# A Fourier layer and a two-layer net on one core: half tiles first, eight weight parts converted in eleven steps, and zero products in TensorE's first pauses

## The chip, the core and the metric

The kernel runs on one NeuronCore of a Trainium2 chip. Its engines run side by side, each through its own list of instructions, and wait for each other on semaphores: TensorE (PE, matmuls; PEld is its weight load), VectorE (DVE), ScalarE (ACT), GpSimd (POOL) and SyncE (SP, which here only issues DMAs). The metric is the device time of one execution in microseconds. Less is better. PE can be granted half its clock; the profile shows the granted share.

## The reference

```python
X = np.fft.rfft(x, axis=1)                       # x: 8 x 3008 x 256
Yr = Xr @ w_r - Xi @ w_i + b_r
Yi = Xr @ w_i + Xi @ w_r + b_i
Yr = np.sign(Yr) * np.maximum(np.abs(Yr) - 0.01, 0.0)    # Yi likewise
y = np.fft.irfft(Yr + 1j * Yi, n=3008, axis=1)
h = y.reshape(24064, 256) @ w_in                 # w_in: 256 x 2048
out = np.maximum(h, 0.0) ** 2 @ w_out            # w_out: 2048 x 256
```

Everything is in float32 but w_in and w_out, which come as float64 and are converted on the chip. A product in full float32 precision is made of two-part numbers: each operand is split into a rounded part and a rest (fp32r), and three products are added; where the operands are still plain fp32, PE runs two passes instead, and the trace has two records for one matmul.

## The kernel before

The length 3008 is 47 × 64. A batch's transform has four stages: **fwd**, 13 products of x with a 120 × 120 matrix (`Fwd`, `Fwd2`, `Fwd32`), whose results go to DRAM (`s1`); **pairs** (or single **units** for batch 0), which load 64 rows of them as `ka`, multiply by a matrix `kbb` (`kb`), mix with w_r and w_i, shrink, and multiply back with `kk` (`kcm`), with results to DRAM (`s3`) as `kuh` and `kul`; **back**, which loads `du` from `s3` and multiplies by `dx_sb` (`dm_sb` for batch 0) to make the tokens' inputs; and **tokens**, sums and splits of these into `yt`. Each batch has six token tiles of 504 or 500 tokens (`HALF`, half of it each).

The net of a tile runs in 8 **steps** of two hidden blocks (`Step`): `first` and `second` make seven products in `psh` instead of eight (a scheme of sums in the manner of Strassen, so win holds seven blocks each in two parts), DVE makes `mu`, `mv` and `mc` from them (L556, L108), ACT squares and rounds (`mg`, L104), POOL makes the rest of `mg` (L111), and `out` two half-steps later adds 12 products into `pso`. Half-steps are the unit of time of a planner (`Plan`): the other batches' transforms are groups with a wanted half-step, a number of half-steps for which they hold one of two PSUM banks (`psfa`, `psfb`), and groups that they follow; `placed` gives each the first fitting half-step. Within a half-step the order of the code is kept on each engine by `then`.

Ahead of the steps, in the order of the program: the **ring** (batch 0's fwd, seven `Fwd32` with folds of x on DVE and POOL), then the mix weights' loads, then 24 **units** in a pipeline (`r` counts them) with their back products, while DVE converts parts of the weights; then seven fwd products of batch 1 (`second`), then back products of tile 0 and 1 and two more of `second`. The 16 **parts** of w_in and w_out are each loaded (`dst`) and converted on ACT and DVE by `begin`, `sign`, `least`, `top`, `power`, `times`, `plus` (L155 to L183), and then split into two parts, for w_in together with sums of two parts (`ds`). Parts 0 to 10 go beside the units (`PACED`), parts 12 and 13 just behind (`BEHIND`), and parts 11, 14 and 15 (`LATE`) together with the sums of parts 12 and 13 in **turns**: what `late_parts` lists is put out on ACT and DVE at the start of each of the first seven steps.

SP's queue is in the order of the code; there is a rule that a load is issued only after a named instruction (`issue_after`). The loads of a unit (`Unit32.load`) are `ka`, and for each fourth unit `kbb` and `kk` (for four units) behind it.

Of the kernel before, what the change touches and what calls it, by code (L numbers as in the profile page):

```python
# [11 lines left out]
F32 = mybir.dt.float32  # L12
# [28 lines left out]
MAIN = {  # L41
    "xs": 1, "xe": 1, "du": 2, "kv": 1, "kp": 1, "kq": 1, "ksh": 1, "ksl": 1, "kxl": 1, "kxh": 1, "kyh": 1, "kyl": 1, "ke": 1, "kb": 1, "yr": 1,
    "ms": 1, "mp": 1, "mu": 1, "mv": 1, "mc": 3, "nam": 1,
}
CONV = ("big", "small", "dw", "ds")
SIDE = ("xs", "ka", "kb", "kcm", "kxh", "kxl", "kyh", "kyl", "kp", "kq", "ke", "kv", "ksh", "ksl", "kuh", "kul", "ku")
# [14 lines left out]
def fnet_moe(ctx: ExitStack, tc, x, w_r, w_i, b_r, b_i, w_in, w_out, bm, cm, dx, a32, c32, d32, out):  # L61
# [58 lines left out]
    nc.sync.dma_start(am32, a32)  # L120
    pool.memset(lam, -LAM)
    w32 = []


    def load_mix_weights():
# [18 lines left out]
    class Double:  # L144
# [7 lines left out]
        def begin(self):  # L152
            self.f = T("df", [128, 512], I32, tag="small")
# [3 lines left out]
        def sign(self):  # L157
            return dve.tensor_scalar(
# [98 lines left out]
    class Fwd:  # L257
# [28 lines left out]
        def run(self):  # L286
# [3 lines left out]
            self.ev = T("xe", [M1, 1, 2, D], F32)  # L290
# [15 lines left out]
    class Pair:  # L306
# [73 lines left out]
        def back(self, g):  # L380
            ps = bank([128, 512])
            for n, (j, r) in enumerate(((0, self.sh), (1, self.sh), (0, self.sl))):
                then(
                    pe, pe.matmul, ps[:, :D], self.cm[:, g, j * 128:(j + 1) * 128], r[:, g],
                    start=n == 0, stop=n == 2,
                )
            store_back(self.b, self.g + g, ps[:, :D])


    class Fwd2(Fwd):  # L390
        kept = None

# [8 lines left out]
        def run(self):  # L401
# [7 lines left out]
            self.ev = T("xe", [M1, 1, 2, D], F32, tag=self.kept or ("xe" if self.q >= PRE else "xf"))  # L409
# [5 lines left out]
    class Fwd32(Fwd):  # L415
# [6 lines left out]
        def mm(self):  # L422
            n = self.n
            self.ps, self.folds = [], []
            for t, eng in enumerate((dve, dve if self.alone else pool)):
# [3 lines left out]
                nc.tensor.matmul(ps[:M1, :n], am32[:, t], u[:, :n], start=True, stop=True)  # L429
# [8 lines left out]
    kk = [None, None]  # L438

    class Unit32:  # L440
        def __init__(self, b, g):
            self.b, self.g = b, g

        def load(self):
            self.a = T("ka", [128, D], F32)
            self.get = nc.sync.dma_start(self.a, s1[self.b][self.g, :N1].rearrange("n t c -> (n t) c"))
            if self.g % 4 == 0:
                with tc.issue_after(units[self.g - 4].get.ins if self.g else ring[-1].last.ins):
                    for j, (name, src) in enumerate((("kbb", bm), ("kk", c32))):
                        kk[j] = T(name, [128, 4, 128], F32)  # L450
                        nc.sync.dma_start(kk[j], src[:, self.g:self.g + 4])
            self.m, self.k = kk[0][:, self.g % 4], kk[1][:, self.g % 4]

        def fwd(self):
            self.ps = ps = bank([128, 2, 256])
            for c in range(2):
                nc.tensor.matmul(  # L457
                    ps[:, c, 0:128], self.a[:, c * 128:(c + 1) * 128], self.m, start=True, stop=True
# [22 lines left out]
        def back(self):  # L481
            self.ps = ps = bank([128, 512])
            nc.tensor.matmul(ps[:, :D], self.k, self.v, start=True, stop=True)  # L483
# [74 lines left out]
    class Tokens:  # L558
# [16 lines left out]
        def split(self, k):  # L575
            y, h = raw[self.t], self.h
            eng = pool if k == 1 else self.eng
            if k == 0:
                yts[self.t] = [
                    T(f"yt{j}", [128, 7 * HM], F32R)[:, :7 * h].rearrange("p (j h) -> p j h", j=7) for j in range(2)  # L580
# [12 lines left out]
    acc = {}  # L593

    class Step:
# [8 lines left out]
        def first(self):  # L604
# [10 lines left out]
            eng = dve if self.t else act  # L615
# [5 lines left out]
        def second(self):  # L621
# [7 lines left out]
            if self.t:  # L629
# [12 lines left out]
        def out(self, j):  # L642
            t, h, f = self.t, self.h, 2 * self.n + j
            if f == 0:
                acc[t] = [bank([128, 512], f"pso{d}") for d in range(2)]

            for d, k in ((0, 0), (0, 1), (1, 0), (1, 1), (0, 2), (1, 2)):
# [4 lines left out]
                    start=f == 0 and k == 0, stop=f == NF - 1 and k == 2,  # L652
                )
            if f == NF - 1:
                b, c0, _ = tiles[t]

# [361 lines left out]
```

## Time and profile before

| what | us |
| --- | --- |
| three runs | 2602.91, 2604.4, 2605.41 (median 2604.4) |
| profiled execution: time | 2605.25 |
| profiled execution: span of its records | 2603.5 |
| PE busy (granted clock 0.996) | 2567.4 |
| DVE, ACT, POOL busy | 1731.9, 1329.7, 1622.1 |

A row of a timeline has start and duration of instructions of one kind (us), the engine, the line, what is made from what (tile names without numbers), the shape, the count, and in brackets the idle time ahead of it with what ended it. A row of waits has the engine and line that waited, what it waited for, total us, number and longest.

### The profile page before, as it was taken

Reading aid. Unit: us, or ns where it says so; the run is one execution under the profiler, and the core shown is the slowest. Engines: PE = TensorE matmul, PEld = TensorE weight load, DVE = VectorE, ACT = ScalarE, POOL = GpSimd, SP = SyncE. Lnnn points to the kernel's source line nnn. Section 1 sums busy time; section 2 is a strip of 40 time slices with the busy share of each in tenths; the row PEclk is TensorE's granted clock in tenths of the full one; section 3 lists DMA queues with packets and bytes.
Section 4 is the critical chain, followed back from the end, with each engine's and each line's share of the span. In section 5 each row is a group of like instructions: output and inputs, shape, how many; then the busy total and the mean of one; then the engine's idle time right before and its main releaser. Section 6 shows DMA issues by size and latency. Waiting matters only on the chain.

```text
span 2603.5 us, 46919 instructions
## 1 busy us (share of the span) xinstructions
PE 2567.4 (99%) x16940; PEld 2349.0 (90%) x16940; DVE 1731.9 (67%) x3724; ACT 1329.7 (51%) x2100; POOL 1622.1 (62%) x1614
## 2 busy tenths in 40 slices
PE   7999999999999999999999999999999999999999
PEld 5889999999999999999999999999999999999998
DVE  6786666676757666576666666667666677755554
ACT  5655454554545545555455554545455555545453
POOL 1066676666766766667666766676666666656664
PEclk8999999999999999999999999999999999999999
DMA  8623333233323333233322343223332232211010
GB/s 266 218 76 101 107 92 92 84 114 103 97 70 117 99 105 94 76 97 99 112 86 82 103 119 101 74 80 107 104 110 76 67 96 92 62 47 53 21 35 17
DMA packets 184569, 244.21 MB, mean 94 GB/s; under 512 B 20910, under 2 KB 129958, under 8 KB 184338
## 3 DMA queue, kind: packets, MB, share of 16 engines
q1 hardware_dynamic: 171442, 217.10, 27.5%
q0 software_dynamic: 12896, 24.11, 3.8%
q8 instruction: 135, 2.21, 0.4%
q14 instruction: 96, 0.79, 0.1%
HBM read 143.74 MB, written 97.39 MB: 93 GB/s over the span
## 4 chain that ended last, share of the span: by engine, by line
PE 96%; DVE 2%; DMA 1%; issue 1%; POOL 0%; ACT 0%; SPq 0%; POOLq 0%; DVEq 0%; ACTq 0%
PE pso L556 39%; PE psh L556 35%; PE psfa L556 9%; PE psfb L556 9%; PE psf L471 2%; PE psf L429 1%; DMA s<-xe 1%; DVE mc L108 0%; PE psf L457 0%; PE psf L483 0%; DVE df L166 0%; PE psf L556 0%; DVE dw L177 0%; DVE da L163 0%; DVE mv L556 0%
## 5 line engine op out<-in xcount | busy, mean ns | idle before, releaser
L111 POOL TENSOR_TENSOR mg<-mc,mg 128x500 fp32r<-128x500 f32 (+1 forms) x768 | 962.8, 1275 | 671.0 <-ACT mg L104 617.7
L556 PE MATMUL pso<-mg,wout 128*128 128x500 f32 (+1 forms) x4608 | 1156.9, 391 | 0.5 <-ACT mg L104 0.2
L556 PE MATMUL psh<-yt,win 128*128 128x250 f32 (+1 forms) x8064 | 1052.3, 281 | 3.3 <-DVE mc L108 3.2
L556 PEld LDWEIGHTS psh<-yt,win 128*128 128x128 f32 x8064 | 992.4, 189 | 17.5 <-DVE mc L108 2.7
L556 PEld LDWEIGHTS pso<-mg,wout 128*128 128x128 f32 x4608 | 823.8, 188 | 135.6 <-POOL mg L111 2.6
L556 ACT ACTIVATE mc<-mc 128x1000 f32<-128x1000 f32 (+1 forms) x384 | 400.7, 1044 | 577.7 <-DVE mc L108 576.4
L108 DVE CUSTOM_DVE_ANT_0 mc<-psh,mv 128x500 f32<-128x500 f32 (+3 forms) x768 | 420.4, 548 | 383.3 <-PE psh L556 340.1
L104 ACT CAST mg<-mc 128x1000 fp32r<-128x1000 f32 (+1 forms) x384 | 396.5, 1032 | 22.4 <-ACT mc L556 1.8
L556 DVE TENSOR_TENSOR mv<-psh,mu 128x500 f32<-128x500 f32 (+1 forms) x384 | 260.8, 679 | 36.9 <-PE psfa L556 0.9
L105 DVE COPY mp<-psh 128x250 f32<-128x250 f32 (+1 forms) x376 | 157.1, 418 | 87.8 <-PE psh L556 67.4
L556 DVE TENSOR_TENSOR mu<-psh,mp 128x250 f32<-128x250 f32 (+1 forms) x384 | 160.5, 418 | 16.7 <-ACT mp L104 5.8
L268 POOL TENSOR_TENSOR xs<-xt 120x256 f32<-120x256 f32 x156 | 112.5, 743 | 80.8 <-PE psfa L556 34.0
L108 DVE CUSTOM_DVE_ANT_0 mc<-psh,mp 128x250 f32<-128x250 f32 (+1 forms) x384 | 156.7, 408 | 0.0
L111 POOL TENSOR_TENSOR ksl<-kv,ksh 128x512 fp32r<-128x512 f32 x84 | 108.9, 1297 | 16.3 <-ACT ksh L104 9.5
L111 POOL TENSOR_TENSOR yt<-ms,yt 128x500 fp32r<-128x500 f32 (+1 forms) x94 | 107.5, 1144 | 5.3 <-ACT yt L104 5.2
L111 POOL TENSOR_TENSOR yt<-yr,yt 128x500 fp32r<-128x500 f32 (+1 forms) x95 | 89.6, 943 | 10.4 <-ACT yt L104 5.5
L111 POOL TENSOR_TENSOR ms<-yr 128x250 f32<-128x250 f32 (+1 forms) x94 | 65.8, 707 | 46.3 <-DVE yr L543 41.9
L373 DVE TENSOR_TENSOR kv<-psfa,ke 64x256 f32<-64x256 f32 x148 | 62.3, 421 | 37.6 <-PE psfa L556 27.8
L373 DVE TENSOR_TENSOR kv<-psfb,ke 64x256 f32<-64x256 f32 x188 | 79.1, 421 | 12.4 <-PE psfb L556 7.0
L111 POOL TENSOR_TENSOR kyl<-kp,kyh 128x256 fp32r<-128x256 f32 x84 | 62.5, 744 | 33.2 <-ACT kyh L104 32.4
L104 ACT CAST ksh<-kv 128x512 fp32r<-128x512 f32 x84 | 52.0, 619 | 59.1 <-DVE kv L111 59.1
L556 PE MATMUL psfb<-wx,kxh 128*128 128x256 f32 x352 | 76.4, 280 | 0.0
(153 smaller groups left out, 2772.4 us busy)
## 6 DMA issues: line engine op xcount, KB each, us to landing
du<-s SPq DMA_DIRECT2D x112, 256.0 KB, 3.1
ka<-s SPq DMA_DIRECT2D x84, 256.0 KB, 3.5
kcm<-cm_in POOLq DMA_DIRECT2D x84, 256.0 KB, 3.3
s<-kuh SPq DMA_DIRECT2D x168, 128.0 KB, 1.8
s<-kul SPq DMA_DIRECT2D x168, 128.0 KB, 2.1
s<-xe SPq DMA_DIRECT2D x85, 240.0 KB, 2.4
xt<-x_in SPq DMA_DIRECT2D x84, 240.0 KB, 3.5
out<-mo SPq DMA_DIRECT2D x64, 250.0 KB, 3.0
```

Source lines behind the costliest of these rows:

```text
L104: return act.copy(out=out, in_=in_)
L105: return eng.tensor_copy(out=out, in_=in_)
L108: return dve._custom_dve(TENSOR_ADD_SAT, out=out, in0=in0, in1=in1, s0=_float(0x7F7FFFFF), s1=0.0)
L111: return eng.tensor_tensor(out=out, in0=a, in1=b, op=ALU.subtract)
L268: return eng.tensor_tensor(out=out[:, :n], in0=self.xt[:, :n, 0], in1=self.xt[:, :n, 1], op=(ALU.add, ALU.subtract)[t])
L373: dve.tensor_add(out=v[64 * r:64 * r + 64, g], in0=ps[gs], in1=self.e[gs, r])
L429: nc.tensor.matmul(ps[:M1, :n], am32[:, t], u[:, :n], start=True, stop=True)
L471: nc.tensor.matmul(ps[:, :D], self.x[:, c, js], w32[j][:, c], start=n == 0, stop=n == 3)
L556: last_of[eng] = op(*args, **kwargs)
```

## The change

* **Zeros.** `awake(n)` issues n matmuls of a tile of zeros into an unused bank: 6 ahead of the ring, 16 behind the ring's last product.
* **First loads.** The first `kbb` is issued ahead of the first `ka`; `kk` and the next `kbb` come behind each fourth `ka`.
* **In place.** The results of `Fwd` and `Fwd2` are copied from PSUM over their own input tile and stored from there; the buffers `xe` and `xf` go, and an input tile is loaded again only when that store has landed.
* **Parts.** `PACED` is 8 parts, spaced 2.75 units instead of 2.5; `BEHIND` is parts 8, 9 and 10 (of which only `dw` is made there); `LATE` is 12, 13, 11, 14, 15, and the turns also hold the sums of two pairs of parts and the split of part 10, in eleven steps instead of seven. The conversion's memory is given back after these.
* **Steps.** Tile 0's steps 0 to 3, then tile 1's 0 to 3, tile 1's 4 to 7, tile 0's 4 to 7, then tile 2 on as before. Tile 0's sums after its first half are copied by ACT into `part` and added by DVE at its end. The `yt` of both tiles have buffers of their own. For tile 1 too ACT instead of DVE copies `p1`, and its `finish` is put out a step later.
* **Second batch.** Its pairs start at half-step 22.2 (was 14.8) with 4.6 between them (was 5.0), and both back products of a pair share a bank; the third batch's fwd starts at 22.4 with 5.5 between (was 16 and 6). A tile's `du` loads are put behind the last back product of the batch that they read.

```diff
-    "a32": 1, "b32": 1, "w320": 1, "w321": 1, "big": 4, "small": 4, "ds": 1, "dw": 3, "ka": 6, "xe": 7, "x2": 4,
-    "kv": 4, "kc": 2, "kn": 2, "kx": 3, "ku": 4, "psf": 6, "x6": 7, "xf": 4, "nam": 1,
+    "a32": 1, "b32": 1, "w320": 1, "w321": 1, "big": 4, "small": 3, "ds": 1, "dw": 3, "ka": 6, "xe": 7, "x2": 4,
+    "kv": 4, "kc": 2, "kn": 2, "kx": 3, "ku": 4, "psf": 6, "x6": 7, "nam": 1, "zero": 1,
+    def awake(n, after=None):
+        ps = bank([128, 512])
+        for _ in range(n):
+            with tc.issue_after(after.ins) if after else nullcontext():
+                after = pe.matmul(ps[:, :D], zero[:, :128], zero, start=True, stop=True)
+        return after
...
+        Unit32.matrix(0, "kbb", bm)
...
-            self.ev = T("xe", [M1, 1, 2, D], F32)
+            self.ev = self.xt
             copy(act, self.ev[:, 0], ps[:M1])
...
-        def back(self, g):
-            ps = bank([128, 512])
-            for n, (j, r) in enumerate(((0, self.sh), (1, self.sh), (0, self.sl))):
-                then(
-                    pe, pe.matmul, ps[:, :D], self.cm[:, g, j * 128:(j + 1) * 128], r[:, g],
-                    start=n == 0, stop=n == 2,
-                )
-            store_back(self.b, self.g + g, ps[:, :D])
+        def back(self, *gs):
+            ps = bank([128, 2, D])
+            for g in gs:
+                for n, (j, r) in enumerate(((0, self.sh), (1, self.sh), (0, self.sl))):
+                    then(
+                        pe, pe.matmul, ps[:, g], self.cm[:, g, j * 128:(j + 1) * 128], r[:, g],
+                        start=n == 0, stop=n == 2,
+                    )
+                store_back(self.b, self.g + g, ps[:, g])
...
-            self.ev = T("xe", [M1, 1, 2, D], F32, tag=self.kept or ("xe" if self.q >= PRE else "xf"))
+            self.ev = self.xt
...
+        @staticmethod
+        def matrix(g, name, src):
+            m = T(name, [128, 4, 128], F32)
+            nc.sync.dma_start(m, src[:, g:g + 4])
+            for u in units[g:g + 4]:
+                setattr(u, name, m[:, u.g % 4])
+
         def load(self):
             self.a = T("ka", [128, D], F32)
             self.get = nc.sync.dma_start(self.a, s1[self.b][self.g, :N1].rearrange("n t c -> (n t) c"))
-            if self.g % 4 == 0:
-                with tc.issue_after(units[self.g - 4].get.ins if self.g else ring[-1].last.ins):
-                    for j, (name, src) in enumerate((("kbb", bm), ("kk", c32))):
-                        kk[j] = T(name, [128, 4, 128], F32)
-                        nc.sync.dma_start(kk[j], src[:, self.g:self.g + 4])
-            self.m, self.k = kk[0][:, self.g % 4], kk[1][:, self.g % 4]
+            with tc.issue_after(self.get.ins):
+                if self.g % 4 == 3:
+                    self.matrix(self.g - 3, "kk", c32)
+                    if self.g + 1 < G:
+                        self.matrix(self.g + 1, "kbb", bm)
...
+                slot = (self.t + (self.t > 1)) % 2
...
-            eng = dve if self.t else act
+            eng = dve if self.t > 1 else act
...
+            ends = (NF // 2 - 1, NF - 1) if t == 0 else (NF - 1,)
+            begin, end = f == 0 or f - 1 in ends, f in ends
...
+                whole = f == NF - 1
+                o = T("mo", [128, 4 * HM], F32, tag="ms" if whole else "part")[:, :4 * h].rearrange("p (d h) -> p d h", d=2)
                 for d in range(2):
-                    then(act, copy, act, o[:, d], acc[t][d][:, :2 * h])
-                    nc.sync.dma_start(out[b, :, d, c0:c0 + 2 * h], o[:, d])
+                    if t in part:
+                        then(dve, dve.tensor_add, out=o[:, d], in0=acc[t][d][:, :2 * h], in1=part[t][:, d])
+                    else:
+                        then(act, copy, act, o[:, d], acc[t][d][:, :2 * h])
+                    if whole:
+                        nc.sync.dma_start(out[b, :, d, c0:c0 + 2 * h], o[:, d])
+                if not whole:
+                    part[t] = o
...
+            if close:
+                back = plan.group(at + end, lambda u=u: u.back(0, 1), 2, [(shrunk, 5)])
+                continue
...
+            if t > 1:
+                plan.job(at, k.load, [(behind, 1)])
...
+    awake(6)
...
+    awake(16, ring[-1].end)
...
-    PACED, BEHIND, LATE = 11, (12, 13), (11, 14, 15)
+    PACED, BEHIND, LATE = 8, (8, 9, 10), (12, 13, 11, 14, 15)
...
-    paced = [(n, (5 * n) // 2) for n in range(PACED)]
-    loads = [(k - 4, parts[n]) for n, k in paced] + [(20 + j, parts[n]) for j, n in enumerate(BEHIND)]
+    paced = [(n, (11 * n) // 4) for n in range(PACED)]
+    loads = [(max(k - 4, 3 * n - 3) if n < 2 else k - 4, parts[n]) for n, k in paced] + [(17 + j, parts[n]) for j, n in enumerate(BEHIND)]
...
-    steps = [Step(t, n) for t in range(len(tiles)) for n in range(NF // 2)]
+    half = NF // 4
+    steps = [Step(t, n + at) for t, at in ((0, 0), (1, 0), (1, half), (0, half)) for n in range(half)]
+    steps += [Step(t, n) for t in range(2, len(tiles)) for n in range(NF // 2)]
...
-    convert(12, units[-1])
-    parts[13].bits(units[-1])
-    parts[13].join()
+    plan.job(0.6, soon[2].load)
+    for n in BEHIND:
+        parts[n].bits(units[-1])
+        parts[n].join()
...
-    def late_parts(pair, v11, v14, v15):
-        rows, add = pair.rows, pair.add
+    def late_parts(v10, v12, v13, v11, v14, v15):
+        p2, p3 = (Sums(n, parts[4 * n:4 * n + 2]) for n in (2, 3))
+        h2, h3, l2, l3, a2, a3 = (
+            [(op, getattr(p, name), j) if name == "rows" else (p.add, j) for j in range(4)]
+            for op, name, p in (
+                (high, "rows", p2), (high, "rows", p3), (low, "rows", p2), (low, "rows", p3),
+                (None, "add", p2), (None, "add", p3),
+            )
+        )
         return (
-            (((high, rows, 0), (high, rows, 1), (v11.begin,)), (*((add, j) for j in range(4)), (v11.sign,))),
-            (((high, rows, 2), (high, rows, 3)), ((low, rows, 0), (low, rows, 1), (v11.least,), (v11.top,))),
-            (((v14.begin,),), ((low, rows, 2), (low, rows, 3), (v11.power,), (v11.times,))),
-            ((), ((v11.plus,), (v14.sign,), (v14.least,), (v14.top,))),
-            (((high, v11.rows), (v15.begin,)), ((v14.power,), (v14.times,), (v14.plus,), (v15.sign,))),
-            (((high, v14.rows),), ((low, v11.rows), (v15.least,), (v15.top,), (v15.power,))),
-            ((), ((low, v14.rows), (v15.times,), (v15.plus,))),
+            ((h2[0], h2[1], (high, v10.rows), (v12.begin,)), (*a2, (v12.sign,), (v12.least,))),
+            ((h2[2], h2[3]), (l2[0], l2[1], (low, v10.rows), (v12.top,))),
+            (((v13.begin,),), (l2[2], l2[3], (v12.power,), (v12.times,))),
+            ((), ((v12.plus,), (v13.sign,), (v13.least,), (v13.top,), (v13.power,))),
+            (((v11.begin,),), ((v13.times,), (v13.plus,), a3[0], a3[1], a3[2])),
+            ((h3[0], h3[1]), (a3[3], l3[0], (v11.sign,), (v11.least,), (v11.top,))),
+            ((h3[2], h3[3], (v14.begin,)), (l3[1], l3[2], (v11.power,), (v11.times,))),
+            ((), (l3[3], (v11.plus,), (v14.sign,), (v14.least,))),
+            (((high, v11.rows), (v15.begin,)), ((v14.top,), (v14.power,), (v14.times,), (v14.plus,))),
+            (((high, v14.rows),), ((low, v11.rows), (v15.sign,), (v15.least,), (v15.top,))),
+            ((), ((low, v14.rows), (v15.power,), (v15.times,), (v15.plus,))),
...
-                first, step, end = 14.8, 5.0, 7.1
-                run = None
+                first, step, end = 22.2, 4.6, 7.1
...
-            first, step = (2.6, 7.0) if b else (16.0, 6.0)
+            first, step = (2.6, 7.0) if b else (22.4, 5.5)
```

The order that results is shown at three places. **SP's queue between ring and units**, `ka` being a unit's input and `dst` a part of the weights. Before:

```order
L446 DMA ka<-s_0_60 128x256
L451 DMA kbb<-bm_in 128x512
L451 DMA kk<-c_in 128x512
L446 DMA ka<-s_0_60 128x256
L150 DMA dst<-w_in_in 128x1024
L446 DMA ka<-s_0_60 128x256 x2
```

And with the change:

```order
L456 DMA kbb<-bm_in 128x512
L462 DMA ka<-s_0_60 128x256 x3
L161 DMA dst<-w_in_in 128x1024
L462 DMA ka<-s_0_60 128x256
L456 DMA kk<-c_in 128x512
L456 DMA kbb<-bm_in 128x512
```

kbb moved ahead of the first ka, three ka stand together, and kk moved behind the fourth.

**DVE in the eighth step** (from `mu` on; the names are those of the steps, the conversion's and, with k, the transform's). Before:

```order
L556 TENSOR_TENSOR mu<-psh_1703,mp 128x252
L556 TENSOR_TENSOR mv<-psh_1704,mu 128x504
L108 ISA mc<-psh_1704,mv 128x252
L108 ISA mc<-psh_1705,mv 128x504
L111 TENSOR_TENSOR kxl<-psfb,kxh 128x512
L339 TENSOR_TENSOR kp<-psfb,kq 128x256
L108 ISA mc<-psh_1706,mp 128x252
```

And with the change:

```order
L571 TENSOR_TENSOR mu<-psh_1693,mp 128x252
L571 TENSOR_TENSOR mv<-psh_1694,mu 128x504
L109 ISA mc<-psh_1694,mv 128x252
L112 TENSOR_TENSOR win_84<-ds,win_83 128x2x256
L194 TENSOR_TENSOR dw<-dw,df 128x512
L169 TENSOR_SCALAR df<-dst 128x512
L174 TENSOR_SCALAR da<-da 128x512
L109 ISA mc<-psh_1695,mv 128x504
L109 ISA mc<-psh_1696,mp 128x252
```

Where a pair's first results were taken, four operations of a turn now stand between the mc of the step.

**PE at the last back product of the second batch** (`ksh`, `ksl`), near step 41, and the first product that reads its result (`dx_sb`). Before, 60 rows lie between the last `ksl` and the first `dx_sb` (first the rows at the back product, then those at its reader):

```order
L556 MATMUL pso_4225<-mg_4540,wout_85 128x500
L556 MATMUL psfb<-ksh,kcm 128x256 x2
L556 MATMUL psfb<-ksl,kcm 128x256
L556 MATMUL psh_4630<-yt_3756,win_83 128x250
L556 MATMUL psh_4630<-yt_3756,win_84 128x250
```

```order
L556 MATMUL pso_4224<-mg_4696,wout_85 128x500
L556 MATMUL pso_4225<-mg_4696,wout_85 128x500
L556 MATMUL psfa<-dx_sb,du 128x2x94 x2
L556 MATMUL psfa<-dx_sb,du 128x188
L556 MATMUL pso_4224<-mg_4695,wout_85 128x500
```

With the change, 33 rows lie between:

```order
L571 MATMUL pso_4161<-mg_4575,wout_85 128x500
L571 MATMUL psfa<-ksh,kcm 128x256 x2
L571 MATMUL psfa<-ksl,kcm 128x256
L571 MATMUL psfa<-ksh,kcm 128x256 x2
L571 MATMUL psfa<-ksl,kcm 128x256
L571 MATMUL pso_4160<-mg_4574,wout_85 128x500
```

```order
L571 MATMUL pso_4161<-mg_4671,wout_86 128x500
L571 MATMUL pso_4160<-mg_4672,wout_85 128x500
L571 MATMUL pso_4161<-mg_4672,wout_85 128x500
L571 MATMUL psfb<-dx_sb,du 128x2x94 x2
L571 MATMUL psfb<-dx_sb,du 128x188
```

Both back products of the last pair now stand together, and half as many rows lie between them and the product that reads them.

More of the change, by code (lines that the diff above doesn't have):

```diff
@@ L428, in mm @@
                 ps = bank([128, 2, D])
-                nc.tensor.matmul(ps[:M1, :n], am32[:, t], u[:, :n], start=True, stop=True)
+                self.end = nc.tensor.matmul(ps[:M1, :n], am32[:, t], u[:, :n], start=True, stop=True)
                 self.ps.append(ps)
@@ L577, in split @@
             eng = pool if k == 1 else self.eng
-            if k == 0:
+            if self.t not in yts:
+                slot = (self.t + (self.t > 1)) % 2
                 yts[self.t] = [
-                    T(f"yt{j}", [128, 7 * HM], F32R)[:, :7 * h].rearrange("p (j h) -> p j h", j=7) for j in range(2)
+                    T(f"yt{j}", [128, 7 * HM], F32R, tag=f"yt{j}{slot}")[:, :7 * h].rearrange("p (j h) -> p j h", j=7)
+                    for j in range(2)
                 ]
@@ L726, in fwd_tasks, with back_tasks @@
             plan.group(at + 0.3, f.run)
-    def back_tasks(t, start, first=False):
+    def back_tasks(t, start, first=False, behind=None):
         b, c0, h = tiles[t]
@@ L739, in back_tasks @@
         v = Tokens(t)
-        rest = [(7.1 + j, lambda j=j: v.sums(j)) for j in range(2)]
-        rest += [(9.1 + 1.2 * j, lambda j=j: v.split(j)) for j in range(4)]
+        sums, splits, order, end = {
+            1: ((5.5, 6.1), (6.6, 7.3, 8.0, 8.7), (0, 2, 3, 1), 9.8),
+            2: ((8.0, 8.8), (11.5, 12.6, 13.7, 14.8), (2, 3, 0, 1), 16.0),
+        }.get(t, ((7.1, 8.1), (9.1, 10.3, 11.5, 12.7), range(4), 14.6))
+        rest = [(at, lambda j=j: v.sums(j)) for j, at in enumerate(sums)]
+        rest += [(at, lambda j=j: v.split(j)) for j, at in zip(order, splits)]
         if len(k.spans) > 1:
-            rest.append((14.6, k.put))
+            rest.append((end, k.put))
         for at, run in rest:
@@ L838, in load_late @@
             chain[nc.sync] = p.get
+    soon = back_tasks(1, -1.6)[0]
+    for k in soon[:2]:
+        k.load()
     load_late()
@@ L847, in fnet_moe @@
         run()
-    second[PRE].kept = "mc"
     for c, f in enumerate(second[PRE:PRE + 2]):
@@ L882, in fnet_moe @@
             if b == 0:
-                first, step, end = 14.8, 5.0, 7.1
-                run = None
+                first, step, end = 22.2, 4.6, 7.1
+                old = run = None
                 for q in range(PRE + 2, J):
-                    plan.job(1.5 * (q - PRE - 2), second[q].load, [(run, 1)])
-                    run = plan.group(1.5 + 1.5 * (q - PRE - 2), second[q].run, 1, [(run, 3)])
-                plan.job(first - 0.6, pairs[1][0].load)
-            pair_tasks(pairs[b + 1], zero + first, step, end, b == 0)
+                    at = 1.5 * (q - PRE - 2)
+                    plan.job(max(at - 1.5, 0.0), second[q].load, [(old, 1)])
+                    old, run = run, plan.group(at + 1.5, second[q].run, 1, [(run, 3)])
+                plan.job(first - 0.7, pairs[1][0].load)
+            behind = pair_tasks(pairs[b + 1], zero + first, step, end, b == 0)
         if b + 2 < B:
-            first, step = (2.6, 7.0) if b else (16.0, 6.0)
+            first, step = (2.6, 7.0) if b else (22.4, 5.5)
             fwd_tasks(b + 2, zero + first, step)
@@ L895, in fnet_moe @@
             t = b * len(HALF) + j + 1
-            if t < len(tiles):
-                back_tasks(t, zero + NF * j + 0.5)
+            if 1 < t < len(tiles):
+                last = behind if t % len(HALF) == 0 else None
+                back_tasks(t, zero + NF * j + (0.5 if t > 2 else -3.0), behind=last)
     todo = plan.placed()
@@ L911, in fnet_moe @@
             steps[n].first()
-            if n and not steps[n - 1].t:
+            if n and steps[n - 1].t < 2:
                 steps[n - 1].finish()
```

31 lines of the change are left out of this document (14 added, 17 removed), and 3 rows, old and new, of the table MAIN.

## The prediction

> **What bounds the kernel now.** I read the page's engine lines and the chain first, then PE's waits, then PE in stretches of time, and the three places where PE stands still.
>
> ```profile
> PE 2567.4 (99%) x16940; PEld 2349.0 (90%) x16940; DVE 1731.9 (67%) x3724; ACT 1329.7 (51%) x2100; POOL 1622.1 (62%) x1614
> PE 96%; DVE 2%; DMA 1%; issue 1%; POOL 0%; ACT 0%; SPq 0%; POOLq 0%; DVEq 0%; ACTq 0%
> ```
>
> TensorE (PE) is busy 99% of 2603.5 us and the change takes no product away. A gain can come only out of PE's idle and half-clocked time, and new idle time is a loss. Where that time is, PE's waits say (engine, line, what was waited for, total us, times, longest).
>
> ```profile
> PE psf L457 <- DMA kbb<-bm_in: 9.1, 1, 9.1
> PE psf L429 <- DVE x L268: 6.8, 1, 6.8
> PE psh L556 <- DVE mc L108: 3.2, 5, 0.9
> PE psf L483 <- DVE kv L111: 3.1, 1, 3.1
> PE psfb L556 <- ACT xe L104: 2.7, 2, 2.4
> PE psf L457 <- DMA ka<-s: 1.3, 1, 1.3
> ```
>
> Five of the six are before 125 us: 6.8 at the start, 9.1 and 1.3 between the ring and the units, 3.1 at the last unit, 2.7 before the steps. The sixth (mc) is in the first steps. The stretches show what the waits leave out (us of the stretch, busy us of PE, PEld, DVE, ACT, POOL, granted clock, DMA).
>
> ```profile
> 40.00:60.00 20.00, 20.00 (x108) 17.99 (x108) 18.70 (x43) 16.81 (x47) 0.00 (x0) 1.00 0.79 230
> 115.00:120.00 5.00, 4.32 (x20) 4.32 (x21) 0.68 (x2) 2.72 (x9) 0.53 (x1) 0.55 0.54 195
> 124.48:187.00 62.52, 58.22 (x362) 50.22 (x361) 52.74 (x78) 32.14 (x56) 35.72 (x32) 1.00 0.30 88
> ```
>
> From 40 us the units keep PE full, with DVE at 18.70 of 20 close behind. At 115 the clock was 0.55 after a pause. In the first eight steps (124.48 to 187) PE's records cover 58.22 of 62.52 us; giving each matmul there the time that its like takes where PE waits for nothing, its work is 54.5, so these steps lose **8.0 us**.
>
> **The change part by part.** All is reckoned against the profiled execution, 2605.25 us; the median, 2604.4, is 0.85 lower, and I subtract that at the end.
>
> *Zeros and loads in the first break.* First PE's and SP's rows there (start, duration, engine, line, operation, count).
>
> ```profile
> 19.44 2.12 PE L429 MATMUL psf<-x,am 120*120 120x512 f32 x6
> 30.66 1.20 PE L457 MATMUL psf<-kbb,ka 128*128 128x128 f32 x4 [9.10 <-DMA kbb<-bm_in]
> 33.20 1.20 PE L457 MATMUL psf<-kbb,ka 128*128 128x128 f32 x4 [1.34 <-DMA ka<-s]
> 34.19 3.29 PE L471 MATMUL psf<-w,kx 128*128 128x256 f32 x8
> 37.31 0.61 PE L457 MATMUL psf<-kbb,ka 128*128 128x128 f32 x4
> ...
> 27.15 0.34 SPq L446 DMA_DIRECT2D ka<-s  x1
> 27.54 0.43 SPq L451 DMA_DIRECT2D kbb<-bm_in  x1
> 28.49 0.43 SPq L446 DMA_DIRECT2D ka<-s  x1
> ```
>
> A unit leaves 14 records, ten of 256 columns and four of 128. The 108 records of 40 to 60 us make it 20 × 14 / 108 = 2.59 us, so 256 columns cost 0.216. A zero matmul is two such records, 0.43 us. The six before the ring lie in the 6.8 us wait for the first x: 0. The sixteen behind it are 6.9 us at full clock, from 21.56 to 28.4 and thus inside the 9.1 us wait, which ends later: 0 as well. What they buy is clock. Before, the eight mix records took 3.29 us where ten such 256-column slots take 2.16 (eight: 1.73), so the first units ran at about half speed until 37. With the zeros the clock should still be up when the units begin.
>
> kbb is now issued ahead of the first ka instead of behind it, so it no longer decides; the first ka, issued at 27.15, does, and I take 29.6 for the first unit. The second and third ka follow at once (two 0.43 us issues earlier than 28.49), which takes the 1.3 us wait. Counted to the point where three forwards and the first mix are done, 37.92 before: 29.6 + 3 × 0.43 + 1.73 is 32.6, and I put 33.2, for a little waiting on the ACT and DVE copies that a first unit has nothing to cover with. That is −4.7; less 0.9 for a chance that the half-empty stretch up to 31 still drops the clock: **−3.8** (bounds −5.3 and −1.3, the latter if the clock falls all the same and only kbb and ka move).
>
> [...]
>
> *The tail of the units.* Eight parts instead of eleven are converted beside the units, so DVE is no longer late at the last one: the 3.1 us kv wait falls to about 1.4 (the bare chain of a last unit): **−1.8** (0 to −3.1).
>
> *The second break.* PE's and ACT's rows:
>
> ```profile
> 112.73 0.58 PE L556 MATMUL psfa<-dm_sb,du 96*128 96x94 f32 x4
> 115.68 1.17 PE L556 MATMUL psfb<-dm_sb,du 96*128 96x94 f32 x4 [2.37 <-ACT xe L104]
> 120.06 2.62 PE L556 MATMUL psfa<-xt,am 120*120 120x256 f32 x6
> 115.05 0.59 ACT L104 COPY xe<-psf 120x512 f32<-120x512 f32 x1 [2.59 <-DMA s<-xe]
> ```
>
> ACT's copies waited until a store had freed one of four buffers, and PE waited for ACT. Copied in place there is no buffer to wait for: the 2.4 go. The half clock that followed (four records took 1.17 after the pause and 0.58 ahead of it; the six of 120.06 took 2.62 where 1.30 is full rate) cost 3.3 up to 122.4 and goes too, the pause being gone. About 0.8 of copy latency stays: **−4.9** (−5.7 to −2.4). The in-place buffers of the main loop are reloaded only when their store has landed; the transforms of a batch stand 5.5 half-steps (some 14 us) apart and have two buffers, which covers a store of 2.4 us (the page's median): 0. If that cover went it would be some 2 us once a transform, on SP.
>
> *The turns.* A turn is what DVE converts in a step; there are eleven, of about 2.43 us at DVE's undisturbed rates, instead of seven of about 2.2. How long they really take:
>
> ```profile
> L163 DVE TENSOR_SCALAR da<-da 128x512 f32<-128x512 f32 x11 | 4.6, 419 | 0.0
> L177 DVE SCALAR_TENSOR_TENSOR dw<-dst,da 128x512 f32<-128x512 uint32 x12 | 8.2, 684 | 0.0
> ...
> L163 DVE TENSOR_SCALAR da<-da 128x512 f32<-128x512 f32 x3 | 4.5, 1490 | 0.0
> L177 DVE SCALAR_TENSOR_TENSOR dw<-dst,da 128x512 f32<-128x512 uint32 x3 | 4.5, 1504 | 0.1
> ...
> 140.54 2.99 POOL L111 TENSOR_TENSOR mg<-mc,mg 128x504 fp32r<-128x504 f32 x2 [4.01 <-ACT mg L104]
> ...
> 138.49 0.42 DVE L556 TENSOR_TENSOR mu<-psh,mp 128x252 f32<-128x252 f32 x1 [0.49 <-ACT mp L104]
> 146.36 0.42 DVE L556 TENSOR_TENSOR mu<-psh,mp 128x252 f32<-128x252 f32 x1 [0.49 <-ACT mp L104]
> 177.50 0.41 DVE L556 TENSOR_TENSOR mu<-psh,mp 128x252 f32<-128x252 f32 x1
> 181.89 0.42 DVE L556 TENSOR_TENSOR mu<-psh,mp 128x252 f32<-128x252 f32 x1
> ```
>
> The first two rows are DVE by shape from 40 to 110 us, the next two from 125 to 185: the same operations go from 0.42 to 1.49 and from 0.68 to 1.50, because POOL, still during the units, works 2.99 us a step on mg in the steps. A step with a turn lasts 7.87 (138.49 to 146.36), one without 4.39 (177.50 to 181.89). The six full turn steps of before are 7.1 to 8.3 us long: 3.2 of step work, the turn, and **1.8 of stretching**. So the new turn steps cost 3.2 + 2.43 + 1.83 = 7.46, and about 8.2 in the two that have a tile's tokens on POOL beside them. The last of eleven ends, from the first psh on, 1.5 + 6.2 (the first step) + 8 × 7.46 + 2 × 8.2 + 0.8 = 84.6 us. PE's work up to there, counted in the new order, is 70.5. These steps lose 14 us where the old ones lost about 7 to the same point: **+7.1**. What keeps PE's work above 54.5 is that the steps between hold tiles 0's and 1's halves and the transforms. Bounds: with no stretching a step is 5.6, below the 6.4 of PE work that it has, and the loss of before goes too (−6); with every operation held for all of POOL's 2.99 it is 8.6 and the loss grows to +17. The first eleven steps are like the seven measured ones in both engines' mixes, so I take their 1.8, and +3 to +11 for the range.
>
> [...] The rows agree that the stretching appears only beside POOL; a single-input operation (da, 1.49) is stretched as well. [...]
>
> *The denser second batch.* Its pairs start at slot 22.2 with step 4.6 instead of 14.8 and 5.0, and its last backward product stands 33 matmul records ahead of the first token product that needs it, 60 before. The rows of before at that place:
>
> ```profile
> 407.25 0.28 PE L556 MATMUL psfb<-ksl,kcm 128*128 128x256 f32 x1
> 408.43 1.36 SPq L303 DMA_DIRECT2D s<-kul  x1
> 412.06 3.27 SPq L118 DMA_DIRECT2D du<-s  x6
> 409.82 2.88 PE L556 MATMUL pso<-mg,wout 128*128 128x500 f32 x12
> 412.54 2.59 PE L556 MATMUL psh<-yt,win 128*128 128x250 f32 x21
> 414.97 1.53 PE L556 MATMUL pso<-mg,wout 128*128 128x500 f32 x6
> 416.33 0.48 PE L556 MATMUL psfa<-dx_sb,du 128*128 128x188 f32 x3
> ```
>
> From the product's end (407.53) to the load's issue (412.06) there are 4.5 us, and the load needs the page's 3.1 to land plus its own issue: 7.6 to 8.4. Before, PE had 8.8 us of other work and waited for nothing. Now 12 pso and 21 psh are 414.97 − 409.82 = 5.15. It waits about **+2.6** (1.8 to 3.9), once: the third batch is placed as before. The pairs' closer spacing puts more work into the same steps: **+0.4** (0 to 1).
>
> *The halves of tiles 0 and 1* cost two ACT copies and two DVE additions of 0.42 at the end of tile 0, and p1 on ACT instead of DVE for tile 1; ACT is at 51% and PE has other tiles' products meanwhile: 0, and 0.8 once if nothing covers.
>
> Sum: −3.8 − 1.8 − 4.9 + 7.1 + 2.6 + 0.4 = −0.4; on 2605.25 and less 0.85, **2604.0 us**.
>
> **The rivals.** *Front gain kept* (faster): PE's products hide the turns, since the work of two half tiles and the transforms stands beside them. It needs a stretching under about 1 us a step; then the +7.1 is about 0 and the time 2597. Against it: the seven measured steps stretch by 1.8. For it: POOL has less transform work early, as the pairs start later. *Turns stretch as in the token steps* (slower): every turn step lasts 8.2, because the eleven turns reach into the steps where POOL also splits tokens. That is 8 × 0.74 = 5.9 more: 2610; the point from which it decides, that is over 0.2% or 2609.6, is 0.7 us more a step. With the chain of step 41 at its long end it is 2611. For it: the two such steps of before; against it: most of the eleven have no tokens. *The zeros don't hold the clock* (the change does not do what it says): they read one constant tile, and if they count for nothing the first break gives −1.3 instead of −3.8 and the second is as forecast: 2606.5, inside no change. [...]
>
> **How the numbers follow.** A measurement of this kernel can tell about 0.2%, 5.2 us, from no change (2599.2 to 2609.6). Forecast with its two clock variants: 0.57. Front gain kept or better: 0.23. Turns longer: 0.20. The bounds of the single terms hold within some 4 us of the sum for the likeliest case, 2600 to 2609; the range reaches to both others, 2596 to 2612. Faster 0.23, same 0.55, slower 0.22.
>
> **What would show it.** Right: the first unit near 29.6 with a granted clock of 1.00 from 25 to 40; no ACT wait for a store between 100 and 116; first psh near 114; DVE at about 7.5 us from mu to mu in eleven steps with PE waiting for mc; a du wait of some 2.6 us near 400 us. Wrong: mu to mu at 6 us, or PE idle at other places after 200 us than that one, such as waits for ka or for the reloaded xt.

## The result and the profile after

The changed kernel took **2627.03 us** (median of 4 runs, 2624.16 to 2628.24) against 2604.32 before (4 runs): ratio 1.0086, 95% interval 1.0068 to 1.0103. It is slower by 22.7 us, where no change was forecast and 2612 was the end of the range.

The profiled execution is the fastest of the four, 2624.16 us with a span of 2622.3, so 18.8 over the span of before; what follows explains these 18.8. The other three executions are 2.5 to 4.1 us longer, at a granted clock of 0.998 to 0.999 where the profiled one has 1.000. The page's engine lines:

```profile
PE 2584.6 (99%) x16984; PEld 2355.0 (90%) x16984; DVE 1740.3 (66%) x3718; ACT 1330.6 (51%) x2108; POOL 1623.3 (62%) x1615
```

44 more PE records are the 22 zero products. PE's waits, after (engine, line, waited for, total us, times, longest):

```profile
PE psfb L571 <- DVE kul L112: 6.9, 6, 1.6
PE psfa L571 <- DVE kul L112: 5.6, 6, 1.0
PE psh L571 <- DVE mc L109: 4.6, 10, 1.2
...
PE psfa L571 <- DMA xt<-x_in: 1.6, 1, 1.6
PE psf L472 <- DMA ka<-s: 1.6, 1, 1.6
PE psfb L571 <- DMA du<-s: 1.3, 2, 1.1
PE psfb L571 <- POOL ksl L112: 1.3, 2, 0.9
PE psf L498 <- DVE kv L112: 1.3, 1, 1.3
```

The long early waits of before (kbb 9.1, x 6.8, xe 2.7) are gone. At the head stands one that was not there and that the prediction does not have: **kul**, twelve times, once for each pair of the second batch. All but one of the twelve lie between 225 and 450 us. Before, PE's waits from 187 to 450 us were these two alone:

```profile
PE psfa L556 <- POOL ksl L111: 0.7, 2, 0.4
PE psfb L556 <- DVE kv L111: 0.7, 1, 0.7
```

The place of one kul wait in PE's timeline (start, duration, engine, line, operation, count, idle before):

```profile
244.99 0.40 PE L571 MATMUL psfa<-ksh,kcm 128*128 128x256 f32 x2
245.23 0.28 PE L571 MATMUL psfa<-ksl,kcm 128*128 128x256 f32 x1
246.53 0.50 PE L571 MATMUL psfa<-ksh,kcm 128*128 128x256 f32 x2 [1.02 <-DVE kul L112]
246.87 0.28 PE L571 MATMUL psfa<-ksl,kcm 128*128 128x256 f32 x1
```

These are the two back products of a pair of the second batch. The second one writes the other half of the same bank, and it waits for DVE. ACT's and DVE's rows for the first one:

```profile
245.54 0.37 ACT L105 CAST kuh<-psfa 128x256 fp32r<-128x256 f32 x1 [0.34 <-PE psfa L571]
...
244.94 0.42 DVE L571 TENSOR_TENSOR mu<-psh,mp 128x250 f32<-128x250 f32 x1
245.46 0.68 DVE L571 TENSOR_TENSOR mv<-psh,mu 128x500 f32<-128x500 f32 x1
246.06 0.41 DVE L112 TENSOR_TENSOR kul<-psfa,kuh 128x256 fp32r<-128x256 f32 x1
```

The first product ends at 245.51, ACT copies it, DVE has a step's mv ahead of its kul, and PE goes on at 246.53, after kul's end at 246.47. Meanwhile the products of the step stand queued behind it on PE.

To see where the rest is I counted, as in the prediction, what PE *loses*: time passed less the time that its instructions up to there take where PE waits for nothing (the zeros, 9.5 us, count as lost, since they compute nothing). By stretch, us:

| | before | after | both_first | turns7 | front_xt3 |
| --- | --- | --- | --- | --- | --- |
| to the first step's first product | 32.6 | 22.5 | 22.4 | 26.4 | 27.0 |
| steps with turns, to 187 (before, front_xt3), 199 (turns7), 227 | 8.0 | 16.9 | 15.6 | 5.9 | 6.4 |
| from there to 449 | 2.5 | 18.8 | 7.0 | 8.2 | 3.4 |
| from 449 to the end | 9.2 | 12.9 | 12.8 | 12.7 | 9.5 |
| sum | 52.3 | 71.1 | 57.8 | 53.2 | 46.3 |

(The last three are experiments below; one of the twelve kul waits lies in the second row.) 71.1 − 52.3 is the 18.8: by row −10.1, +8.9, +16.3 and +3.7. The forecast had −10.5, +7.1, +3.0 and 0 for the same rows. The first row keeps what was forecast; the third row, with kul, is what was not.

### The profile page after: what moved, and what is told of

Same layout as the page of the kernel before. It is cut to its first block, busy times and chain, and to the rows that moved or that the text cites. A ratio compares the mean times of both kernels' runs of the same rounds, so it can differ in the third digit from the quotient of the medians.

```text
span 2622.3 us, 47003 instructions
## 1 busy us (share of the span) xinstructions
PE 2584.6 (99%) x16984; PEld 2355.0 (90%) x16984; DVE 1740.3 (66%) x3718; ACT 1330.6 (51%) x2108; POOL 1623.3 (62%) x1615
## 4 chain that ended last, share of the span: by engine, by line
PE 94%; DVE 2%; POOL 2%; DMA 1%; issue 1%; ACT 1%; SPq 0%; POOLq 0%; ACTq 0%; DVEq 0%
PE pso L571 39%; PE psh L571 34%; PE psfb L571 9%; PE psfa L571 9%; PE psf L486 2%; POOL mg L112 1%; DMA x<-x_in 1%; PE psf L571 0%; PE psf L498 0%; PE psf L472 0%; DVE mc L109 0%; POOL yt L112 0%; DVE kul L112 0%; POOL ms L112 0%; DMA s<-xe 0%
## 5 line engine op out<-in xcount | busy, mean ns | idle before, releaser
L279 POOL TENSOR_TENSOR xs<-xt 120x256 f32<-120x256 f32 x156 | 112.9, 746 | 78.6 <-DVE mp L106 22.5
L384 DVE TENSOR_TENSOR kv<-psfa,ke 64x256 f32<-64x256 f32 x192 | 80.8, 421 | 13.1 <-PE psfa L571 9.0
L384 DVE TENSOR_TENSOR kv<-psfb,ke 64x256 f32<-64x256 f32 x144 | 60.7, 422 | 39.9 <-PE psfb L571 33.0
L105 ACT COPY dy<-psfa 128x188 f32<-128x188 f32 (+3 forms) x116 | 36.6, 315 | 76.8 <-PE psfa L571 76.3
```

The lines of the kernel that those rows point to most:

```text
L105: return act.copy(out=out, in_=in_)
L279: return eng.tensor_tensor(out=out[:, :n], in0=self.xt[:, :n, 0], in1=self.xt[:, :n, 1], op=(ALU.add, ALU.subtract)[t])
L384: dve.tensor_add(out=v[64 * r:64 * r + 64, g], in0=ps[gs], in1=self.e[gs, r])
```

## The experiments

Fourteen kernels ran, in four groups; those of one group shared the runs of the kernel before on their chip, whose medians lie between 2604.49 and 2605.05. Ratios are to before, with 95% intervals. Times and gains are medians; the profiled execution of a kernel can lie some us off its median, and so the table can differ from them.

**both_first.** The changed kernel, with the copies behind both products:

```diff
             for g in gs:
                 for n, (j, r) in enumerate(((0, self.sh), (1, self.sh), (0, self.sl))):
...
-                store_back(self.b, self.g + g, ps[:, g])
+            for g in gs:
+                store_back(self.b, self.g + g, ps[:, g])
```

> The changed kernel, with both back products of a pair issued ahead of the copies that read them, still in one PSUM bank. Theory A (the second product waits until ACT and DVE have read the first one out of the same bank, 12 waits of about 1.2 us with the refill): those twelve waits go, and the time is 14 us under the changed kernel's, about 2612, still 8 over before (ratio 1.003). Rival B (batch 2's pairs are simply too dense for ACT and DVE from half-step 40 on): PE then waits for kul or kv at the next place, and less than 4 us is gained (ratio 1.007 or more).

2613.66 us, 1.0035 (1.0021 to 1.0048): 13.4 less than the changed kernel. Its PE rows at the same place:

```profile
243.66 0.40 PE L572 MATMUL psfa<-ksh,kcm 128*128 128x256 f32 x2
243.90 0.28 PE L572 MATMUL psfa<-ksl,kcm 128*128 128x256 f32 x1
244.02 0.40 PE L572 MATMUL psfa<-ksh,kcm 128*128 128x256 f32 x2
244.25 0.28 PE L572 MATMUL psfa<-ksl,kcm 128*128 128x256 f32 x1
```

No pause. The bank is still shared; only the order of the program has changed. Theory A holds. One kul wait of 1.2 is left, at a later user of the bank. Whether the second product has to wait for the copies at all, since they read the other half of the bank, no run here asks, and a kernel with the new spacing and a bank for each back product was not run.

**before_joint.** The kernel before with the shared bank alone (with it the two products of a pair stand directly one behind the other, as in the changed kernel):

```diff
+            if close:
+                back = plan.group(at + end, lambda u=u: u.back(0, 1), 2, [(shrunk, 5)])
+                continue
             back = plan.group(at + end, lambda u=u: u.back(0), 1, [(shrunk, 5)])
```

> The kernel before, with only this of the change: both back products of a pair of the second batch share one PSUM bank, the copies of the first standing between them. Its pairs keep their old start and spacing (14.8 and 5.0). Theory A: twelve waits of PE on kul, about 1.0 to 1.2 us each, so 12 to 14 us slower than before (ratio 1.005). Rival B (density): with the old spacing at most 3 us slower.

2627.07 us, 1.0084 (1.0067 to 1.0100): 22.0 slower, more than A's 12 to 14, and far from B. The kul waits are the 13.8 us that A had; ksl and the clock are the excess. Why POOL's ksl comes later here was not looked into. PE's waits in it:

```profile
PE psfa L557 <- DVE kul L111: 10.4, 9, 1.8
PE psfa L557 <- POOL ksl L111: 3.5, 1, 3.5
PE psfb L557 <- DVE kul L111: 3.4, 3, 1.6
PE psfb L557 <- POOL ksl L111: 2.2, 1, 2.2
```

Its timeline of PE at the longest of these:

```profile
387.09 0.56 PE L557 MATMUL psfa<-ksl,kcm 128*128 128x256 f32 x1 [3.47 <-POOL ksl L111]
388.57 0.79 PE L557 MATMUL psfa<-ksh,kcm 128*128 128x256 f32 x2 [0.92 <-DVE kul L111]
```

And the stretches there (the third column from the end is the granted clock):

```profile
385.00:390.00 5.00, 1.99 (x7) 1.70 (x8) 0.42 (x1) 1.93 (x4) 5.00 (x6) 0.71 0.39 142
390.00:395.00 5.00, 5.00 (x24) 4.71 (x23) 2.36 (x5) 0.00 (x0) 0.67 (x2) 0.60 0.42 108
```

Behind the wait of 3.47, with one of 0.92 close after it, the clock fell, to 0.71 and 0.60 in the two stretches of 5 us. So the shared bank alone, put into the kernel before, costs as much as the whole change.

**no_zeros.** The changed kernel without `awake(6)` and `awake(16, ...)`.

> The changed kernel without any zero products. Theory: the zeros hold the clock from 20 to 40 us; without them the first units run at half clock and the time is 2.5 to 4 us longer than the changed kernel's, with a granted clock near 0.6 in 25 to 35 us. Rival (the gain of the first break is that of the loads alone): within 1 us of the changed kernel.

2629.41 us, 1.0097 (1.0082 to 1.0112): 2.4 more than the changed kernel, a little under the expected 2.5 to 4, and the intervals of the two overlap. The clock is clear. The stretch from 25 to 30 us in no_zeros, with a granted clock of 0.50:

```profile
25.00:30.00 5.00, 0.07 (x1) 0.11 (x1) 1.53 (x3) 0.82 (x2) 0.00 (x0) 0.50 0.95 312
```

And in the changed kernel, with 1.00:

```profile
25.00:30.00 5.00, 3.55 (x17) 2.79 (x15) 1.42 (x3) 0.71 (x2) 0.00 (x0) 1.00 0.97 304
```

So the zeros hold the clock. What that is worth is less than the times say: at the first step's first product no_zeros is 1.0 us behind (115.21 for 114.17). What its profiled execution loses beyond that comes later, where PE waits 2.3 us for ACT's xt (to 125.79 us) and where the clock is 0.66 from 416 to 421 us (the changed kernel has 1.00 there); that the zeros prevent this is not shown.

**front_alone, front_loads, front_xt3.** The kernel before with zeros, first loads and in-place copies only; the second loads its inputs of batch 1 where the changed kernel does; the third has also a third buffer:

```diff
 MAIN = {
-    "xs": 1, "du": 2,
+    "xs": 1, "xt": 3, "du": 2,
```

> The kernel before, with only the zeros, kbb ahead of ka, kk behind the fourth ka, and the copies in place; the conversion keeps its 11 parts beside the units and its seven turns, the steps and the second batch their old places. By the trace of the changed kernel, whose first step product starts 10.3 us earlier, the first break gives 4 to 5, the second 5, and the tail of the units nothing here (kv wait stays at 3.1): 8 to 10 us faster than before (ratio 0.9965). Rival: the first steps are bound by DVE's turns and loads of late parts, and what is gained ahead of them is lost there: under 3 us.

> front_alone (it had PE wait 3.3 us for an input of the second batch loaded again only after its store) with the loads of these four inputs at the places of the changed kernel, half a step or more earlier. Theory A (that wait, and what follows it, took 4 to 5 us of the front's gain): 4 to 5 us faster than front_alone, 2599.5 to 2601, faster than before by 0.17% or more. Rival B (the steps bound by DVE's turns take the gain anyhow): like front_alone, within 2 us of before.

> front_loads with three instead of two input buffers, so that the third input of the second batch need not wait for a store. Theory A: PE's wait for xt (3.2 us) goes and the time falls by 3 to 5 us, to 2599.5 to 2601. Rival B (DVE's turns take it): within 1.5 us of front_loads.

front_alone: 2604.15, 0.9997 (0.9988 to 1.0006). front_loads: 2603.96, 0.9997 (0.9988 to 1.0005). Neither got the gain of its theory A: PE waits 3.3 us for the reload of an input in front_alone, and still 3.2 us in front_loads, so that front_loads did not test what this wait costs.

```profile
124.96 1.68 PE L569 MATMUL psfb<-xt,am 120*120 120x256 f32 x6 [3.18 <-DMA xt<-x_in]
...
119.41 0.83 SPq L288 DMA_DIRECT2D s<-xt  x2
121.88 1.05 SPq L118 DMA_DIRECT2D xt<-x_in  x2
```

That is front_loads's timeline of PE and of SP. The third input can be loaded only when the first result, which lies in the same buffer, has been stored, however early the load stands in SP's queue. With a third buffer the wait is gone: **front_xt3: 2598.32 us, 0.9977 (0.9968 to 0.9986)**, 5.6 under front_loads. The same product in front_xt3, then the stretch from 125 to 130 us in front_loads and in front_xt3 (the third column from the end is the clock):

```profile
121.44 1.46 PE L569 MATMUL psfb<-xt,am 120*120 120x256 f32 x6
...
125.00:130.00 5.00, 5.00 (x23) 4.53 (x24) 0.47 (x2) 1.73 (x3) 0.00 (x0) 0.66 0.27 70
125.00:130.00 5.00, 4.38 (x31) 4.12 (x32) 4.64 (x8) 4.11 (x8) 1.88 (x2) 1.00 0.51 142
```

The wait cost more than its 3.2 us: behind it the clock was 0.66 over 5 us, an estimated 1.7 us more (0.34 of 5). So the rivals, which had DVE's turns take the gain, were right in the time and wrong in the cause. front_xt3 is the one kernel here that does all the work and has its interval wholly under before.

**turns7 and light_turns.** both_first with the conversion of before (11 parts beside the units, seven turns); and both_first with four operations of each late part left out.

> both_first with the conversion of before: 11 parts beside the units, two behind, three and one pair of sums in seven turns; the order of the steps, the halves and the second batch as in the changed kernel. Theory A (each turn step is as long as DVE's work, 7.4 us, and four turns fewer save what they lose): the first steps lose 7 us instead of 14.5, the last unit waits for kv 3.1 instead of 1.3: 4 to 6 us under both_first (ratio to before about 1.0015). Rival B (the loss of the first steps is the half tiles and the closer transforms, whatever DVE converts): within 1.5 us of both_first (1.003 or more).

> both_first without four of the seven operations (least, top, power, plus) of the five late parts, so that those weights are not converted: 11 us less of DVE work by undisturbed durations, some 19 at the stretched ones, in eleven steps. Theory A: the steps come out bound by PE or nearly so, 8 to 13 us under both_first (ratio to before 0.9985 to 1.0005). Rival B: within 3 us of both_first.

turns7: 2605.46, 1.0005 (0.9996 to 1.0014), 8.2 under both_first (4.6 in the profiled executions, by the sums of the table). light_turns, whose late weights are thus not converted: 2601.31, 0.9986 (0.9977 to 0.9995), 12.4 under both_first. Both are what A said or more. DVE's turns set the pace of the first eleven steps, as PE's share in the same 85.83 us shows (the first three after the length are busy us of PE, PEld and DVE). In both_first:

```profile
114.17:200.00 85.83, 77.78 (x477) 65.98 (x476) 75.46 (x109) 44.32 (x81) 45.60 (x38) 1.00 0.26 74
```

In light_turns:

```profile
114.17:200.00 85.83, 84.57 (x543) 75.43 (x542) 64.37 (x106) 52.67 (x94) 55.46 (x51) 1.00 0.27 78
```

**step44.** both_first with `first, step, end = 22.2, 4.4, 7.1`.

> both_first with the second batch's pairs 4.4 half-steps apart instead of 4.6, so that 49 instead of 33 rows stand between its last back product and the first product that reads it. Theory A (PE waits there for the store and load of the last pair, 2.5 us): that wait goes, 2 to 3 us under both_first. Rival B (the closer pairs wait as much elsewhere): no difference.

2615.63, 1.0039 (1.0024 to 1.0055), not to be told from both_first, as B said: the du wait is gone, but PE waits for ksl and kv instead, between 200 and 450 us:

```profile
PE psfa L572 <- POOL ksl L112: 3.6, 2, 1.8
PE psfb L572 <- DVE kv L112: 1.5, 2, 0.7
```

**old_pairs and old_pairs_mc.** turns7 with the second batch's old start and spacing and a bank for each back product; and that with one more buffer borrowed from mc.

> turns7 with the second batch's pairs where they were before (start 14.8, 5.0 apart, each back product in a bank of its own) and the third batch's fwd at 16.0 and 6.0: of the change there remain the zeros, the first loads, the copies in place, the order of the steps in halves. Theory A (the dense second batch costs turns7 about 5.5 us from half-step 22 on; the front and the halves keep some 8 us): 5 us under turns7, and 3 to 5 under before (ratio 0.998 to 0.9990), with 3.4 us still lost evenly from the third batch on. Rival B (old pairs run into the steps with turns and tile 1's tokens): no better than turns7.

> old_pairs with one of the second batch's inputs in a buffer of the steps (mc) so that the next one is loaded without waiting for its store. Theory A (copying in place makes a reload wait for a store, 1.6 to 3.3 us at the first steps): 1.5 to 3 us under old_pairs. Rival B (the load is late for other reasons, or the steps are bound by DVE there): no difference.

old_pairs: 2602.32, 0.9992 (0.9983 to 1.0001), 3.1 under turns7: the way that A said, but less, and the intervals of the two overlap. old_pairs_mc: 2605.65, 1.0008 (0.9999 to 1.0016): neither; it is slower by 3.3, and PE waits 1.5 us for an ACT copy of yt ahead of the first steps that old_pairs does not have. Why that wait came was not looked into.

**before_pad, yt_slots, early_yt.** These ask about the last row of the table: in the changed kernel and everything derived from it PE gets through fewer records at the same busy time, with no wait to see. From 500 to 2500 us, before:

```profile
500.00:2500.00 2000.00, 1996.78 (x13400) 1839.38 (x13399) 1333.32 (x2916) 1018.74 (x1550) 1308.62 (x1302) 1.00 0.30 89
```

And after:

```profile
500.00:2500.00 2000.00, 1996.81 (x13375) 1837.46 (x13374) 1332.65 (x2910) 1016.85 (x1548) 1305.40 (x1301) 1.00 0.30 89
```

25 records at about 0.15 us are 3.7 us, for 3.4 by the count of losses (9.1 and 12.5). Some 2.0 of these lie between one pso product and the next: from start to start they are 229.2 ns apart in the mean before, and 229.8 after. The tiles `mg` lie elsewhere in the memory of the changed kernel. before_pad shifts tiles by 512 bytes; yt_slots gives front_loads the yt buffers of the change, and so its place of mg; early_yt gives old_pairs's tiles out in another order, which brings mg back:

```diff
-            if self.t not in yts:
+            for t in (0, 1) if self.t == 0 else (self.t,):
+                if t not in yts:
...
```

> The kernel before with an unused tile of 512 bytes a partition in the memory of the main part, so that later tiles lie 512 bytes further. Theory A (the changed kernel's even extra loss of 3.4 us from the third batch on comes from where tiles lie): that stretch (450 to 2590 us) loses some us more or less than the 9.2 of before. Rival B (place doesn't matter, or not at this offset): 9.0 to 9.7 us, and the time of before.

> front_loads with only this added: each tile's yt parts have a buffer of their own name, as in the changed kernel, so that the mg tiles lie at 161,600 and up in each partition's memory (bytes), as in the changed kernel and all its variants, instead of 177,792. Same instructions otherwise. Theory A (the even extra loss from the third batch on is where mg lies): from 500 to 2500 us the loss is 12.3 to 12.6 us instead of 9.1 to 9.7, and the time 3 us over front_loads, near 2607. Rival B (it comes from the order or the number of waits of the changed kernel): 9.1 to 9.7 us, the time of front_loads.

> old_pairs with tile 1's yt buffers given out together with tile 0's, ahead of the mg tiles, which then lie at 175,744 instead of 161,600. Theory A: the loss from 500 to 2500 us falls from 12.5 to about 9.3 us, and the time by 3 us to about 2599. Rival B: as old_pairs, 2602.

Lost from 500 to 2500 us: before_pad 9.25 (B), yt_slots 10.3 (neither: a third of the effect), early_yt 12.0 (B). Times: before_pad 2604.83 (1.0002, 0.9992 to 1.0012), yt_slots 2606.06 (1.0004, 0.9995 to 1.0013), early_yt 2602.58 (0.9993, 0.9984 to 1.0002). The place of mg is not the cause, or not alone. It stays open.

## Why the prediction was wrong, point by point

* **First break, tail, second break** (−3.8, −1.8, −4.9; together −10.5): right in the sum. The first step product starts at 114.17 (forecast: near 114), before at 124.48; the losses up to there fall by 10.1. The first unit starts at 30.18 (29.6) and waits 1.6 for ka; the clock is 1.00 from 25 to 40, so the 0.9 set against a fall of it, the author's estimate, was not lost; kv fell to 1.3 (1.4); no copy waits for a store. "In place: 0" was wrong at the first steps: the changed kernel waits 1.6 us there for xt, and front_loads 3.2. The forecast took the spacing of later transforms (5.5 half-steps), and these stand 1.5 apart. Within the first break the split was off, and that the sum came out is in part luck: the zeros were to be worth 2.5 us of the 3.8 (−1.3 without them), and no_zeros is 1.0 us behind at the first step.

* **Turns** (+7.1): right in kind and nearly in size. In both_first these steps lose 7.6 more than before (15.6 for 8.0), in the changed kernel 8.9 with one kul wait. A turn step in the changed kernel's timeline of DVE:

```profile
174.26 0.42 DVE L571 TENSOR_TENSOR mu<-psh,mp 128x252 f32<-128x252 f32 x1 [0.49 <-ACT mp L105]
...
176.65 1.38 DVE L182 TENSOR_SCALAR da<-df 128x512 int32<-128x512 int32 x1
178.07 1.65 DVE L188 SCALAR_TENSOR_TENSOR dw<-dst,da 128x512 f32<-128x512 uint32 x1
...
181.85 0.42 DVE L571 TENSOR_TENSOR mu<-psh,mp 128x252 f32<-128x252 f32 x1 [0.49 <-ACT mp L105]
```

It lasts 7.59 (forecast 7.46), with the stretched 1.38 and 1.65, the first wholly and the second in part beside the 2.81 us that POOL works on mg from 176.37 on. From 40 to 80 us, where POOL does nothing (0.00 us busy), the same two take 0.42 and 0.69. Why they take longer beside POOL is not shown. The ten steps from the second turn on last 7.2 to 8.1, under the 8.6 that the prediction estimated for every operation held for all of POOL's 2.99.

* **The wait at the second batch's end** (+2.6): right. The du wait is 2.5 in both_first; in the changed kernel, where the kul waits bring PE there later, it is 1.3. That undoing it gives nothing (step44) was not foreseen.

* **The denser second batch, "puts more work into the same steps: +0.4"**: this is the step that failed. That both back products of a pair share a bank stands among the changes, but the prediction prices only the spacing; the shared bank has no term, which puts it at nothing. It did not ask what the second product waits for: the copies of the first stand between them in the program, in the same bank, so PE stands still until ACT and DVE have read it, with the step's products queued behind. That is twelve waits, 12.5 us in the waits and 13.4 in the time (both_first). Without them, in both_first, the third row of the table loses 4.5 us more than before, for the 3.0 of the two forecast terms. The prediction's own sign of being wrong, PE idle at other places after 200 us, is what came.

* **After the second batch** (forecast nothing): 3.7 us more are lost, a little at each of many products. Not foreseen, and not explained.

* **The rivals.** "Front gain kept" and "turns longer" were both about the turns, and neither came. No rival had a cause of its own behind the first 220 us but the long end of the du wait, so the range ended where the turns' price ended.

## What to carry to other kernels

When two products are put into one PSUM bank to save a bank or a slot, look at what stands between them in the program. Here the reads of the first did, and the second waited for them, twelve times for 0.9 to 1.6 us, with everything queued behind it; to issue both products first was worth 13.4 us alone. Put a price on an edit that looks like tidying by asking what each of its instructions waits for. And try the parts of a bundle alone: here the front with one more buffer is 6.5 us faster than before, and the bundle, without that buffer and with everything else, 22.7 slower.

## What the hardware showed beyond that

A pause in the middle of the steps can cost more than its length. In before_joint waits of 3.47 and 0.92 us came with a clock of 0.71 and 0.60 in the two stretches from 385 us on. A shorter one came with a slower clock too: one pause of 1.80 us in before_joint, which ended at 269.55, was followed by 0.66:

```profile
270.00:275.00 5.00, 5.00 (x26) 4.69 (x25) 1.03 (x3) 0.98 (x2) 5.00 (x8) 0.66 0.31 101
```

And the same pauses do not always do it. The twelve kul pauses of the changed kernel, 0.9 to 1.6 us, left the clock at 1.00 in the profiled execution. no_zeros has them too, and behind one pair of pauses its clock fell. The changed kernel's rows and stretch first, then those of no_zeros:

```profile
411.20 0.38 PE L571 MATMUL psfb<-ksl,kcm 128*128 128x256 f32 x1 [0.94 <-POOL ksl L112]
412.57 0.50 PE L571 MATMUL psfb<-ksh,kcm 128*128 128x256 f32 x2 [0.98 <-DVE kul L112]
410.00:416.00 6.00, 4.08 (x29) 3.56 (x28) 3.25 (x8) 2.60 (x4) 4.09 (x4) 1.00 0.26 86
...
415.11 0.39 PE L571 MATMUL psfb<-ksl,kcm 128*128 128x256 f32 x1 [0.95 <-POOL ksl L112]
416.47 0.61 PE L571 MATMUL psfb<-ksh,kcm 128*128 128x256 f32 x2 [0.97 <-DVE kul L112]
416.00:421.00 5.00, 4.53 (x23) 4.49 (x24) 2.66 (x6) 1.25 (x2) 2.96 (x3) 0.66 0.36 110
```

The pauses are equal to 0.01 us, and the clock is 1.00 behind one pair and 0.66 behind the other. What decides is not shown here. One trace can therefore give too low a price for such a pause.
